# Block attention and a squared-ReLU network on one Trainium2 core: a third buffer for the loaded sums of weights, key and value sums moved to the fifth chunk, exponentials ahead of the high parts, and the last pair's products in another order

## The chip, the core and the metric

The kernel runs on one core of one Trainium2 chip. The core has a matrix engine (TensorE; PE and, for its weight loads, PEld in the profile), a vector engine (VectorE, DVE), an activation engine (ScalarE, ACT), a general one (GpSimd, POOL) and a queue engine that issues transfers (SyncE, SP). The metric is the device time of one execution in microseconds; lower is better.

## The reference, cut to what matters

```
def _attn_ref(q, k, v):                    # 4 x 8 heads x 768 x 64
    k_sum = k.reshape(B, H, nb, 32, D).max(axis=3)
    v_sum = v.reshape(B, H, nb, 32, D).mean(axis=3)
    scores = [local scores inside |i - j| < 16, scores with k_sum + log(32)] * scale
    a = softmax(scores)                    # 96 local keys of a half tile and 24 sums
    return a @ [v, v_sum]

def _moe_ref(x, w_in, w_out):              # x: 3072 x 512, d_ff 2048
    h = np.maximum(x @ w_in, 0.0)
    return h * h @ w_out
```

The attention's output, 3072 rows of 512, is the input x of the two-layer network. All of it is 32-bit.

## The kernel before, in words

The 3072 rows are 24 attention tiles `g` of 128 rows (six to each of the four batches b), and 12 chunks `c` of 256 rows (two tiles each) for the network. Every network product is made of high and low parts (`w_sb[f]` holds both parts of one 128-wide slice f of the two weight matrices; 16 slices), so a first-layer product of one slice is 12 matmuls of 256 columns (`ffn1`, L414 to L422).

Chunks 0 and 1 and the loading and splitting of the weights run in an order written out by hand (`START`). Chunks 2, 3 and 4 (the "slot" chunks) run in eight slots each (`slot`, L506): a slot computes the first layer of two slices into a PSUM bank (`ph`, bank 4 and 5 in turn), then the second layer of the two slices before (`finish`, 24 matmuls at L463), and squares its own result: ScalarE's ReLU (L426) and square (L432), VectorE's product (L437) and the low part (L440), which reads the bank. Chunks 5 to 11 (the "block" chunks, `chunk_blocks`, L682) compute the second layer by block sums that save products (seven block products, `plain` and `summed`, L618 to L621, 21 matmuls at L630 for a pair of slices, in four accumulating banks `acc`). A pair n has its first layer in slot k of its chunk and its block products two slots later, `ffn2_blocks(n - 2)`; the last two pairs' products stand at the chunk's end.

What the block products need beside the weights:

- sums of blocks of the second matrix, made once in the slot chunks on GpSimd (`sums_t`, `split_t`), stored to DRAM (`t_dram`), and loaded anew for each pair by a transfer on GpSimd's queue (`load_t`, L601) into one of two buffers of `t_ring`, pair n into buffer n % 2. In slot k > 1 `load_t(n)` is issued behind `ffn2_blocks(n - 2)`, which read that buffer last; two more are issued at the chunk's end;
- sums of blocks of the squares (`squares_blocks`, `split_blocks`): ReLU, square and the high part on ScalarE (L426, L640, L642), three subtractions on GpSimd (L644, L649, L650), the low part on VectorE (L651), then the high part of the sums on ScalarE (L655) and their low part on GpSimd (L656). They are written to `sets`.

The attention of the next two tiles is spread over the slots of a chunk by lists of steps. In the slot chunks `period(a)` (L524) gives the steps for tiles a and a + 1: `softmax` is VectorE's masked maximum (L315) and ScalarE's exponential (L323) per head, then sum, reciprocal and normalization (L340, L350, L355), then VectorE transposes into `pT` (`turn`, L368). A period starts with the last slot of a chunk (n = 0) and ends with the seventh of the next (n = 7), where TensorE computes the outputs of both tiles (`outputs`, L386): the first into bank 5, the second into bank 4, which holds the slot's own `ph`. Period a = 6 runs in chunk 2, a = 8 in chunk 3, a = 10 in chunk 4.

The keys' and values' sums of batch b + 1 are formed per pair of heads from transposed copies: `load_kv` (two transfers on SyncE's queue, L193 and L194, into a room of the pool tagged "w", which has one room more than the 16 weight slices) and `sum_k`, `sum_v` (VectorE, L197, L202, L205). Batch 2's four pairs stand in periods 8 and 10, batch 3's in chunks 6 and 7. `place_v` (L210) puts the value sums into the last 32 rows of `v_sb` by VectorE transposes (L214) and GpSimd copies (L219, L220); there is one tile `vsum`.

At a chunk's end `evict_blocks` (L658) joins the four banks into the output: a copy of the first bank's half on ScalarE (L664), additions on VectorE (L665 to L672), and four stores on SyncE's queue (L675, L676).

Of the kernel before, what the change touches and what calls it, by code (L numbers as in the profile page):

```python
# [11 lines left out]
F32 = mybir.dt.float32  # L12
F32R = mybir.dt.float32r
# [4 lines left out]
ALU = mybir.AluOpType  # L18
# [6 lines left out]
P = 128  # L25
# [50 lines left out]
def attn_ffn_kernel(ctx: ExitStack, tc: tile.TileContext, q, k, kt, v, vt, v0, w, consts, out, out_rows):  # L76
# [26 lines left out]
    vsum = const.tile([P, NPAIR, 32], F32, name="vsum")  # L103
# [23 lines left out]
    nc.vector.memset(vsum, 0.0)  # L127

    nc.scalar.activation(vsum[:, 0, 0:1], vsum[:, 0, 0:1], AF.Exp)
# [71 lines left out]
    def sum_v(b, p):  # L201
        nc.vector.tensor_reduce(  # L202
            out=vsum[:, p, 0:NB], in_=kv[b, p][:, S : 2 * S].rearrange("a (n j) -> a n j", j=BLOCK), op=ALU.add, axis=AX.X
        )
        nc.vector.tensor_scalar_mul(vsum[:, p, 0:NB], vsum[:, p, 0:NB], 1.0 / BLOCK)  # L205
# [4 lines left out]
    def place_v(g):  # L210
        dst = v_sb[g % 2][96:128]
        if g % 2 == 0:
            for a in range(4):
                nc.vector.transpose(  # L214
                    out=dst[:, 0, :].rearrange("a (p c) -> a p c", c=128)[:, :, a * 32 : a * 32 + 32],
                    in_=vsum[a * 32 : a * 32 + 32],
                )
        else:
            nc.gpsimd.tensor_copy(out=dst[:, 0, :], in_=v_sb[0][96:128, 0, :])  # L219
        nc.gpsimd.tensor_copy(out=dst[:, 1, :], in_=v_sb[0][96:128, 0, :])  # L220
# [302 lines left out]

    def period(a):  # L524
# [28 lines left out]
        if b + 1 < B and t:  # L553
            for n, p in enumerate(((0, 1), (2, 3))[t // 4]):
                last[2 * n].append(lambda p=p: load_kv(b + 1, p))
                after[2 * n + 2].append(lambda p=p: sum_k(b + 1, p))
                after[2 * n + 2].append(lambda p=p: sum_v(b + 1, p))
# [100 lines left out]
    def evict_blocks(c):  # L658
# [4 lines left out]
        p1, p6 = (acc[0][:, i * CT : (i + 1) * CT] for i in range(2))  # L663
        nc.scalar.copy(out=c11, in_=p1)  # L664
# [8 lines left out]
        o = (c - FROM_BLOCKS) * CT  # L673
        for at, x, y in ((o + P, c11, c12), (o, c21, c22)):
            nc.sync.dma_start(out=out_rows[at : at + P, 0:CT], in_=x)  # L675
            nc.sync.dma_start(out=out_rows[at : at + P, CT:], in_=y)  # L676

    def sharpen(g, half):
        add_eps(g, half, nc.vector)
        inverse(g, half)  # L680

    def chunk_blocks(c):  # L682
# [3 lines left out]
        pairs = ((0, 1), (2, 3))[t // 4] if more and b + 1 < B and t else ()  # L686
        early, late = [[] for _ in range(SLOTS)], [[] for _ in range(SLOTS)]
        if more:
            for h in range(2):
                early[0] += [lambda h=h: sharpen(a, h), lambda h=h: norm(a, h, nc.vector)]  # L690
                early[4].append(lambda h=h: sharpen(a + 1, h))
                early[5].append(lambda h=h: norm(a + 1, h, nc.vector))
# [4 lines left out]
            late[3].append(lambda: softmax(a + 1, 0, 4))  # L697
            early[4].insert(0, lambda: softmax(a + 1, 4, 8))
# [13 lines left out]
        for k in range(SLOTS):  # L712
# [11 lines left out]
            if k > 1:  # L724
                load_t(n)
# [154 lines left out]
    with tc.manual_schedule(engines=None):  # L880
# [17 lines left out]
        for c in range(2, FROM_BLOCKS):  # L898
            for f in range(0, NF, 2):
# [84 lines left out]
```

## Time and profile before

| | |
|---|---|
| runs | 605.14, 608.45, 609.23 us; median 608.45 |
| the profiled execution | 608.73 us, of which the span from the first to the last instruction is 606.7 us |
| mean granted clock of TensorE | 0.99 |
| TensorE matmuls / weight loads | 582.5 / 570.5 us busy |
| VectorE, ScalarE, GpSimd | 397.8, 325.2, 340.3 us busy |
| slot chunks 2 to 4 | about 126 to 269 us of the span |
| block chunks 5 to 11 | about 269 to 600 us |

The profile is of one execution. Its page gives busy time per engine, the chain of work that ended last, and groups of instructions by source line; the trace behind it gives waits, timelines and stretches. A row of a timeline has start, duration, engine, line, operation, names written and read, and in brackets how long the engine had been idle and what ended that. Matmuls are pipelined, so a matmul's own duration (275 ns) is longer than the step from one to the next.

### The profile page before, as it was taken

How to read it: one execution, taken by the hardware profiler on the slowest of the kernel's cores; microseconds unless marked ns; L12 is line 12 of the kernel's file. 1: busy time of each engine (PE TensorE's matmuls, PEld its weight loads, DVE VectorE, ACT ScalarE, POOL GpSimd, SP SyncE). 2: the span in 40 equal slices, each digit the busy share in tenths (PEclk: the TensorE clock that was granted, in tenths of full speed). 3: DMA queues.
4: the chain of work that ended last, by engine and by line, in shares of the span. 5: the costliest groups of instructions: out<-in, count | busy, mean ns of one | idle time of the engine just before them, and what ended most of it. 6: DMA issues, size and time to landing. Idle time of an engine off the chain costs nothing.

```text
span 606.7 us, 15592 instructions
## 1 busy us (share of the span) xinstructions
PE 582.5 (96%) x6263; PEld 570.5 (94%) x6263; DVE 397.8 (66%) x1073; ACT 325.2 (54%) x798; POOL 340.3 (56%) x399
## 2 busy tenths in 40 slices
PE   7799999999999999999999899999999999999993
PEld 6699999999999999999999899899999899999993
DVE  6899897977747948947557756675575565663111
ACT  3899756243454443455554644645655654662540
POOL 2546552016625533657756764774783774874871
PEclk9999999999999999999999999999999999999997
DMA  8999702552328219449566847657547646346252
GB/s 302 348 342 419 311 2 94 160 176 70 122 91 275 76 49 312 123 123 278 175 202 199 293 157 238 226 187 251 181 152 224 214 147 206 120 158 223 76 188 87
DMA packets 41799, 114.91 MB, mean 189 GB/s; under 512 B 3776, under 2 KB 20160, under 8 KB 40192
## 3 DMA queue, kind: packets, MB, share of 16 engines
q1 hardware_dynamic: 31488, 67.79, 32.6%
q0 software_dynamic: 10240, 46.14, 23.6%
q8 instruction: 49, 0.80, 0.5%
q14 instruction: 22, 0.18, 0.1%
HBM read 99.24 MB, written 14.68 MB: 188 GB/s over the span
## 4 chain that ended last, share of the span: by engine, by line
PE 65%; POOL 11%; DMA 10%; ACT 5%; DVE 5%; issue 2%; SPq 1%; POOLq 0%; DVEq 0%; ACTq 0%
PE ph L418 27%; PE o_ps L463 16%; PE s_ps L630 8%; DMA t_ring<-t 7%; PE o_ps L630 5%; PE s_ps L418 3%; POOL q_sb L644 3%; POOL sets L656 3%; PE ph L386 3%; POOL q_sb L649 2%; POOL q_sb L650 2%; PE s_ps L287 2%; DMA w_raw<-in_w 2%; ACT r L426 1%; ACT r L640 1%
## 5 line engine op out<-in xcount | busy, mean ns | idle before, releaser
L418 PE MATMUL ph<-x,w_sb 128*128 128x256 f32 x1608 | 192.1, 276 | 0.0
L418 PEld LDWEIGHTS ph<-x,w_sb 128*128 128x128 f32 x1608 | 187.2, 188 | 0.2 <-issue 0.2
L463 PE MATMUL o_ps<-sq,w_sb 128*128 128x256 f32 x960 | 115.4, 275 | 0.2 <-DVE sq L440 0.2
L463 PEld LDWEIGHTS o_ps<-sq,w_sb 128*128 128x128 f32 x960 | 111.7, 188 | 0.5 <-DVE sq L440 0.4
L651 DVE TENSOR_TENSOR sets<-r,sets 128x384 fp32r<-128x384 f32 x56 | 42.2, 754 | 94.6 <-ACT sets L642 91.3
L368 DVE STREAM_TRANSPOSE pT<-e_sb 32x256 f32<-32x256 f32 x228 | 99.4, 436 | 3.9
L426 ACT ACTIVATE r<-ph 128x512 f32<-128x512 f32 x85 | 50.5, 594 | 64.4 <-PE ph L418 60.4
L323 ACT ACTIVATE e_sb<-e_sb,nmx 128x120 f32<-128x120 f32 x176 | 67.8, 389 | 31.5 <-DVE nmx L315 31.5
L656 POOL TENSOR_TENSOR sets<-q_sb,sets 128x512 fp32r<-128x512 f32 x56 | 72.4, 1292 | 20.8 <-ACT sets L655 19.1
L655 ACT CAST sets<-q_sb 128x512 fp32r<-128x512 f32 x56 | 34.8, 622 | 83.6 <-POOL q_sb L650 83.5
L630 PE MATMUL s_ps<-t_ring,sets 128*128 128x256 f32 x336 | 67.6, 282 | 9.3 <-DMA t_ring<-t 9.1
L644 POOL TENSOR_TENSOR q_sb<-r 128x256 f32<-128x256 f32 x56 | 42.1, 751 | 42.7 <-ACT r L640 40.5
L630 PEld LDWEIGHTS s_ps<-t_ring,sets 128*128 128x128 f32 x336 | 51.3, 189 | 11.7 <-DMA t_ring<-t 11.6
L418 PE MATMUL ph<-sq,w_sb 128*128 128x256 f32 x504 | 61.4, 276 | 0.0
L418 PEld LDWEIGHTS ph<-sq,w_sb 128*128 128x128 f32 x504 | 59.0, 188 | 0.5 <-issue 0.5
L630 PE MATMUL s_ps<-w_sb,sets 128*128 128x256 f32 x336 | 57.2, 279 | 0.0
L601 POOL DMA_DIRECT2D t_ring<-t x56 | 31.8, 567 | 36.0 <-PE o_ps L630 26.0
L263 POOL TENSOR_TENSOR w_raw<-w_raw 128x1024 int32<-128x1024 int32 (+1 forms) x20 | 33.2, 1662 | 30.0 <-DVE w_raw L258 12.6
L630 PE MATMUL o_ps<-w_sb,sets 128*128 128x256 f32 x336 | 49.2, 281 | 0.0
L630 PEld LDWEIGHTS s_ps<-w_sb,sets 128*128 128x128 f32 x336 | 47.3, 190 | 0.0
L630 PEld LDWEIGHTS o_ps<-w_sb,sets 128*128 128x128 f32 x336 | 42.9, 188 | 1.4 <-issue 1.0
L437 DVE TENSOR_TENSOR ph<-ph,r 128x512 f32<-128x512 f32 x32 | 22.3, 697 | 28.7 <-ACT r L426 28.4
(121 smaller groups left out, 904.4 us busy)
## 6 DMA issues: line engine op xcount, KB each, us to landing
t_ring<-t POOLq DMA_DIRECT2D x56, 768.0 KB, 4.5
w_raw<-in_w SPq DMA_DIRECT2D x12, 1024.0 KB, 13.7
v_sb<-in_v SPq DMA_DIRECT2D x22, 384.0 KB, 5.1
t<-f SPq DMA_DIRECT2D x16, 512.0 KB, 3.5
k_sb<-in_k SPq DMA_DIRECT2D x19, 384.0 KB, 6.4
kv<-in_kt SPq DMA_DIRECT2D x16, 384.0 KB, 3.8
q_sb<-in_q SPq DMA_DIRECT2D x24, 256.0 KB, 5.3
kv<-in_vt SPq DMA_DIRECT2D x12, 384.0 KB, 4.6
```

The source lines that it names most:

```text
L263: nc.gpsimd.tensor_tensor(out=lo, in0=hi, in1=lo, op=ALU.add)
L323: nc.scalar.activation(e, e, AF.Exp, bias=nmx[g, half][:, i : i + 1], scale=-1.0, accum_out=sm[g, half][:, i : i + 1])
L368: nc.vector.transpose(out=pT[g % 2][j * 32 : j * 32 + 32, :, i * 32 : i * 32 + 32], in_=e_sb[i * 32 : i * 32 + 32, :, j * 32 : j * 32 + 32],)
L418: nc.tensor.matmul(ph, lhsT=w_sb[f][:, w, cc * P : (cc + 1) * P], rhs=x[c][:, cc, :], start=(n == 0), stop=(n == 3 * NC4 - 1))
L426: nc.scalar.activation(r, ph, AF.Relu)
L463: nc.tensor.matmul(o_ps[c][b][:, i * CT : (i + 1) * CT], lhsT=w_sb[f][:, w, d : d + P], rhs=g_, start=(first and n == 0 and i == 0), stop= ...
L601: nc.gpsimd.dma_start(out=t_ring[n % 2], in_=t_dram[n % SLOTS][:, 1:4])
L630: nc.tensor.matmul(acc[b][:, half * CT : (half + 1) * CT], lhsT=operand(n, x, i), rhs=right(n, name, y), start=(first and b not in banks[: ...
L644: nc.gpsimd.tensor_tensor(out=s_flat[:, 0 : 2 * P].rearrange("p (a b) -> p a b", a=2), in0=r0.unsqueeze(1).to_broadcast([P, 2, P]), in1=r[ ...
L651: nc.vector.tensor_sub(out=l, in0=r[:, P:], in1=h.bitcast(F32))
L655: nc.scalar.copy(out=h, in_=s_flat)
L656: nc.gpsimd.tensor_sub(out=l, in0=s_flat, in1=h.bitcast(F32))
```

## The change

Five edits go together:

- A third buffer for the loaded sums of weights, `t_room`, in the pool's one free room. Pair n uses buffer n % 3, slot k > 1 issues `load_t(n + 1)` instead of `load_t(n)`, and a chunk's end issues the loads n + 2 and n + 3.
- So that the room is free by then, all keys' and values' sums of batches 2 and 3 are formed in the slot chunks: a table `keys_values` names for each period the slots at whose end a pair is loaded; its sums stand two slots later. Batch 3's last pair is summed behind the loop. `vsum` becomes two tiles, one for odd and one for even batches.
- In the block chunks all eight masked maxima of tile a + 1 stand at the end of slot 3, and the eight exponentials in two groups of four in slots 4 and 5, each group ahead of that slot's high part of the sums (L655 before).
- `place_v` copies on ScalarE in the block chunks.
- The last pair's products are ordered so that banks 0 and 1 are complete early, and the last chunk's `evict_blocks` has its own form: seven additions of 256 columns, a store behind each finished quarter, the last of them on ScalarE's queue.

```diff
+    vsums = [const.tile([P, NPAIR, 32], F32, name=f"vsum{i}") for i in range(2)]
...
-    def place_v(g):
+    def place_v(g, eng=nc.gpsimd):
...
-            nc.gpsimd.tensor_copy(out=dst[:, 0, :], in_=v_sb[0][96:128, 0, :])
-        nc.gpsimd.tensor_copy(out=dst[:, 1, :], in_=v_sb[0][96:128, 0, :])
+            copy(eng, dst[:, 0, :], v_sb[0][96:128, 0, :])
+        copy(eng, dst[:, 1, :], v_sb[0][96:128, 0, :])
...
+    keys_values = {
+        6: ((2, 2, 0), (4, 2, 1)), 8: ((0, 2, 2), (2, 2, 3)), 10: ((0, 3, 0), (2, 3, 1), (4, 3, 2), (6, 3, 3)),
+    }
...
-        if b + 1 < B and t:
-            for n, p in enumerate(((0, 1), (2, 3))[t // 4]):
-                last[2 * n].append(lambda p=p: load_kv(b + 1, p))
-                after[2 * n + 2].append(lambda p=p: sum_k(b + 1, p))
-                after[2 * n + 2].append(lambda p=p: sum_v(b + 1, p))
+        for n, i, p in keys_values.get(a, ()):
+            last[n].append(lambda i=i, p=p: load_kv(i, p))
+            if n < 6:
+                after[n + 2] += [lambda i=i, p=p: sum_k(i, p), lambda i=i, p=p: sum_v(i, p)]
...
+                t_ring.append(room(F32R, "t_room")[:, 4 : 4 + 6 * CT].rearrange("p (q i n) -> p q i n", q=3, i=2))
-            nc.gpsimd.dma_start(out=t_ring[n % 2], in_=t_dram[n % SLOTS][:, 1:4])
+            nc.gpsimd.dma_start(out=t_ring[n % 3], in_=t_dram[n % SLOTS][:, 1:4])
...
     def ffn2_blocks(n):
+        if n == n_blocks - 1:
+            passes.sort(key=lambda at: (plain + summed[3:] + summed[:3]).index(at[0]))
...
+        if c == n_c - 1:
+            nc.scalar.copy(out=c21, in_=p1)
+            nc.vector.tensor_add(out=c11, in0=acc[1][:, 0:CT], in1=c21)
+            nc.sync.dma_start(out=to[0], in_=c11)
+            nc.vector.tensor_add(out=c22, in0=p6, in1=c21)
+            nc.vector.tensor_add(out=c12, in0=acc[2][:, 0:CT], in1=c22)
+            nc.vector.tensor_add(out=c12, in0=acc[3][:, 0:CT], in1=c12)
+            nc.sync.dma_start(out=to[1], in_=c12)
+            nc.vector.tensor_add(out=c21, in0=acc[2][:, CT:], in1=c22)
+            nc.vector.tensor_add(out=c22, in0=acc[2][:, 0:CT], in1=c21)
+            nc.sync.dma_start(out=to[3], in_=c22)
+            nc.vector.tensor_add(out=c21, in0=acc[3][:, CT:], in1=c21)
+            nc.scalar.dma_start(out=to[2], in_=c21)
+            return
...
-                early[4].append(lambda h=h: sharpen(a + 1, h))
-                early[5].append(lambda h=h: norm(a + 1, h, nc.vector))
...
-            late[3].append(lambda: softmax(a + 1, 0, 4))
-            early[4].insert(0, lambda: softmax(a + 1, 4, 8))
+            late[3] += [lambda h=h: mask_max(a + 1, h) for h in range(H)]
+            for n in range(2):
+                early[4 + n] += [lambda h=h: exponentials(a + 1, h) for h in range(4 * n, 4 * n + 4)]
+            for h in range(2):
+                early[4 + h] += [lambda h=h: sharpen(a + 1, h), lambda h=h: norm(a + 1, h, nc.vector)]
...
-            for n, p in enumerate(pairs):
-                late[(0, 3)[n]].append(lambda p=p: load_kv(b + 1, p))
-                (late[2] if n == 0 else early[4]).extend([lambda p=p: sum_k(b + 1, p), lambda p=p: sum_v(b + 1, p)])
             if b and t == 0:
-                late[4] += [lambda: place_v(a), lambda: place_v(a + 1)]
+                late[4] += [lambda: place_v(a, nc.scalar), lambda: place_v(a + 1, nc.scalar)]
...
             if k > 1:
-                load_t(n)
+                load_t(n + 1)
...
-        load_t(n + 1)
         load_t(n + 2)
+        load_t(n + 3)
...
+        sum_k(3, 3)
+        sum_v(3, 3)
         softmax(2 * FROM_BLOCKS + 2, 0, H)
-        load_t(0)
-        load_t(1)
+        for n in range(3):
+            load_t(n)
```

Three places of the instruction order, before and after. On VectorE, the end of chunk 4: slots 5, 6 and 7 of its period (product and low part L437 and L440, which are L438 and L441 after the change; transposes into `pT_82`), then the low part of x and the chunk's last slot. Before:

```order
L368 STREAM_TRANSPOSE pT_82<-e_sb 32x8x32 x5
L437 TENSOR_TENSOR ph<-ph,r 128x512
L440 TENSOR_TENSOR sq<-ph,sq 128x512
L368 STREAM_TRANSPOSE pT_82<-e_sb 32x8x32 x7
L437 TENSOR_TENSOR ph<-ph,r 128x512
L440 TENSOR_TENSOR sq<-ph,sq 128x512
L403 TENSOR_TENSOR x<-ph,x 128x4x128 x2
```

The same place after the change, with `ksum_87` and `vsum_84` the sums of batch 3:

```order
L369 STREAM_TRANSPOSE pT_82<-e_sb 32x8x32 x5
L438 TENSOR_TENSOR ph<-ph,r 128x512
L441 TENSOR_TENSOR sq<-ph,sq 128x512
L369 STREAM_TRANSPOSE pT_82<-e_sb 32x8x32 x3
L198 TENSOR_REDUCE ksum_87<-kv 128x24
L203 TENSOR_REDUCE vsum_84<-kv 128x24
L206 TENSOR_SCALAR vsum_84<-vsum_84 128x24
L369 STREAM_TRANSPOSE pT_82<-e_sb 32x8x32 x4
L438 TENSOR_TENSOR ph<-ph,r 128x512
L441 TENSOR_TENSOR sq<-ph,sq 128x512
L404 TENSOR_TENSOR x<-ph,x 128x4x128 x2
```

One pair's sums now stand between the third and the fourth of the seven transposes, ahead of the last slot's product and low part. Chunk 2 has the same new rows there, and another pair's sums two slots before.

On GpSimd, slots 2 to 4 of the first block chunk, chunk 5 (`t2_106` is the DRAM copy of the sums of slice pair 2 of 0 to 7, `t3_107` that of pair 3, and so on; `q_sb2_79` takes the sums of squares). Before:

```order
L650 TENSOR_TENSOR q_sb2_79<-r_84,q_sb2_79 128x128
L601 DMA t_ring_3623<-t2_106 128x1536
L656 TENSOR_TENSOR sets_3676<-q_sb2_79,sets_3676 128x512
L644 TENSOR_TENSOR q_sb2_79<-r_84 128x256
L649 TENSOR_TENSOR q_sb2_79<-r_84,q_sb2_79 128x128
L650 TENSOR_TENSOR q_sb2_79<-r_84,q_sb2_79 128x128
L601 DMA t_ring_3623<-t3_107 128x1536
```

The same slots after the change, where the copy of pair 2 is named `t2_108`, that of pair 3 `t3_109`, that of pair 4 `t4_110`:

```order
L657 TENSOR_TENSOR q_sb2_79<-r_85,q_sb2_79 128x128
L606 DMA t_ring_3649<-t3_109 128x1536
L663 TENSOR_TENSOR sets_3704<-q_sb2_79,sets_3704 128x512
L651 TENSOR_TENSOR q_sb2_79<-r_85 128x256
L656 TENSOR_TENSOR q_sb2_79<-r_85,q_sb2_79 128x128
L657 TENSOR_TENSOR q_sb2_79<-r_85,q_sb2_79 128x128
L606 DMA t_ring_3649<-t4_110 128x1536
```

In each slot the load is that of the next pair; pair 2's has moved ahead of the chunk, behind those of pairs 0 and 1.

On TensorE, the last pair's products (`o_ps` are banks 0 and 1 of the four, `s_ps` banks 2 and 3). Before:

```order
L630 MATMUL o_ps<-w_sb,sets 128x256 x6
L630 MATMUL s_ps<-t_ring,sets 128x256 x3
L630 MATMUL s_ps<-w_sb,sets 128x256 x4
L630 MATMUL s_ps<-t_ring,sets 128x256 x2
L630 MATMUL o_ps<-t_ring,sets 128x256 x2
L630 MATMUL s_ps<-w_sb,sets 128x256 x2
L630 MATMUL s_ps<-t_ring,sets 128x256
L630 MATMUL o_ps<-t_ring,sets 128x256
```

And after:

```order
L637 MATMUL o_ps<-w_sb,sets 128x256 x6
L637 MATMUL s_ps<-t_ring,sets 128x256 x3
L637 MATMUL o_ps<-t_ring,sets 128x256 x3
L637 MATMUL s_ps<-w_sb,sets 128x256 x6
L637 MATMUL s_ps<-t_ring,sets 128x256 x3
```

The last product into banks 0 and 1 was the 21st and is now the 12th.

## Rows read from the trace of the kernel before

**Rows 1.** The page: busy time by engine; a group (count, busy us, mean ns, idle us).
```profile
PE 582.5 (96%) x6263; PEld 570.5 (94%) x6263; DVE 397.8 (66%) x1073; ACT 325.2 (54%) x798; POOL 340.3 (56%) x399
...
L630 PEld LDWEIGHTS s_ps<-t_ring,sets 128*128 128x128 f32 x336 | 51.3, 189 | 11.7 <-DMA t_ring<-t 11.6
```

**Rows 2.** Waits of weight loads: total us, times, longest us.
```profile
PEld s_ps L630 <- DMA t_ring<-t: 11.6, 12, 2.3
```

**Rows 3.** Chain that ended last, chunk 6: start us, us, what.
```profile
345.19 1.77 PE s_ps L630 x9
...
348.24 3.26 PE ph L418 x24
...
352.20 1.02 PE s_ps L630 x9
...
353.90 2.73 PE ph L418 x24
```

**Rows 4.** Two stretches: length, busy us by engine, PEclk, DMA share, GB/s.
```profile
345.84:349.26 3.42, 3.42 (x18) 3.42 (x17) 3.37 (x6) 0.88 (x2) 2.49 (x5) 0.50 0.63 246
20.98:23.36 2.38, 0.38 (x18) 0.12 (x6) 1.68 (x13) 2.20 (x12) 1.96 (x2) 1.00 1.01 384
```

**Rows 5.** Instructions by tile `t_ring`, the line on its transfers.
```profile
DMA to landing us min/median/max: 4.3/4.5/8.6
```

**Rows 6.** Timeline of GpSimd, chunk 6, two successive loads.
```profile
332.91 0.57 POOL L601 DMA_DIRECT2D t_ring<-t  x1
...
337.01 0.57 POOL L601 DMA_DIRECT2D t_ring<-t  x1
```

**Rows 7.** Timeline of the end, all engines.
```profile
594.21 0.84 PE L630 MATMUL o_ps<-w_sb,sets 128*128 128x256 f32 x6
...
597.18 0.62 PE L630 MATMUL s_ps<-t_ring,sets 128*128 128x256 f32 x3 [2.13 <-DMA t_ring<-t]
...
599.34 0.41 PE L630 MATMUL o_ps<-t_ring,sets 128*128 128x256 f32 x1
599.79 0.37 ACT L664 COPY q_sb<-o_ps 128x256 f32<-128x256 f32 x1 [6.55 <-PE o_ps L630]
600.20 0.42 DVE L665 TENSOR_TENSOR q_sb<-o_ps,q_sb 128x256 f32<-128x256 f32 x1 [8.47 <-ACT q_sb L664]
...
603.75 0.46 SPq L676 DMA_DIRECT2D out<-q_sb  x1
```

**Rows 8.** Groups by line and shape from 125 us on: count, busy us, mean ns, idle us.
```profile
L197 DVE TENSOR_REDUCE ksum<-kv 128x24 f32<-128x768 f32 x8 | 7.6, 944 | 0.1
L202 DVE TENSOR_REDUCE vsum<-kv 128x24 f32<-128x768 f32 x8 | 7.5, 942 | 0.0
```

**Rows 9.** Timeline of VectorE (chunks 2, 3) and of TensorE (chunk 2's end).
```profile
149.81 0.70 DVE L437 TENSOR_TENSOR ph<-ph,r 128x512 f32<-128x512 f32 x1 [1.58 <-ACT r L426]
...
163.35 0.69 DVE L440 TENSOR_TENSOR sq<-ph,sq 128x512 fp32r<-128x512 f32 x1
...
164.48 2.08 PE L386 MATMUL ph<-pT,v_sb 128*64 128x64 f32 x64
...
195.81 0.70 DVE L437 TENSOR_TENSOR ph<-ph,r 128x512 f32<-128x512 f32 x1 [1.58 <-ACT r L426]
...
211.69 0.69 DVE L440 TENSOR_TENSOR sq<-ph,sq 128x512 fp32r<-128x512 f32 x1
```

**Rows 10.** Timeline of TensorE and of VectorE, chunk 4's end.
```profile
260.06 2.08 PE L386 MATMUL ph<-pT,v_sb 128*64 128x64 f32 x64
...
260.22 0.69 DVE L440 TENSOR_TENSOR sq<-ph,sq 128x512 fp32r<-128x512 f32 x1
```

**Rows 11.** Timeline of GpSimd and of VectorE, chunk 4.
```profile
247.23 2.41 POOL L587 TENSOR_TENSOR f<-f 128x1024 fp32r<-128x1024 f32 x1 [0.49 <-ACT f L586]
...
247.91 2.25 DVE L355 TENSOR_TENSOR e_sb<-e_sb,sm 128x480 f32<-128x480 f32 x1
```

**Rows 12.** Instructions by tile `kv`, the line on its transfers.
```profile
DMA to landing us min/median/max: 3.0/4.2/14.5
```

More of the change, by code (lines that the diff above doesn't have):

```diff
@@ L102, in attn_ffn_kernel @@
     pT = [const.tile([P, H, P], F32, name=f"pT{i}") for i in range(2)]
-    vsum = const.tile([P, NPAIR, 32], F32, name="vsum")
+    vsums = [const.tile([P, NPAIR, 32], F32, name=f"vsum{i}") for i in range(2)]
     r_sb = const.tile([P, 2, CT], F32, name="r")
@@ L125, in attn_ffn_kernel @@
     bank = [ps_s.tile([P, DM], F32, name=n, tag=f"{n}{i}") for i, n in enumerate(["s_ps"] * 4 + ["ph"] * 2)]
-    nc.vector.memset(vsum, 0.0)
-    nc.scalar.activation(vsum[:, 0, 0:1], vsum[:, 0, 0:1], AF.Exp)
+    for t_ in vsums:
+        nc.vector.memset(t_, 0.0)
+    nc.scalar.activation(vsums[1][:, 0, 0:1], vsums[1][:, 0, 0:1], AF.Exp)
     nc.vector.memset(bank[0][:, 3 * P + NK : 3 * P + NK + 4], 1.0e-9)
@@ L202, in sum_v @@
         nc.vector.tensor_reduce(
-            out=vsum[:, p, 0:NB], in_=kv[b, p][:, S : 2 * S].rearrange("a (n j) -> a n j", j=BLOCK), op=ALU.add, axis=AX.X
+            out=vsums[b % 2][:, p, 0:NB], in_=kv[b, p][:, S : 2 * S].rearrange("a (n j) -> a n j", j=BLOCK), op=ALU.add, axis=AX.X
         )
-        nc.vector.tensor_scalar_mul(vsum[:, p, 0:NB], vsum[:, p, 0:NB], 1.0 / BLOCK)
+        nc.vector.tensor_scalar_mul(vsums[b % 2][:, p, 0:NB], vsums[b % 2][:, p, 0:NB], 1.0 / BLOCK)
     def place_k(g, eng=nc.vector):
         copy(eng, k_sb[g % 2][:, 4], ksums[g // NT % 2].unsqueeze(1).to_broadcast([P, 2, NPAIR, NB]))
-    def place_v(g):
+    def place_v(g, eng=nc.gpsimd):
         dst = v_sb[g % 2][96:128]
@@ L215, in place_v @@
                     out=dst[:, 0, :].rearrange("a (p c) -> a p c", c=128)[:, :, a * 32 : a * 32 + 32],
-                    in_=vsum[a * 32 : a * 32 + 32],
+                    in_=vsums[g // NT % 2][a * 32 : a * 32 + 32],
                 )
         else:
-            nc.gpsimd.tensor_copy(out=dst[:, 0, :], in_=v_sb[0][96:128, 0, :])
-        nc.gpsimd.tensor_copy(out=dst[:, 1, :], in_=v_sb[0][96:128, 0, :])
+            copy(eng, dst[:, 0, :], v_sb[0][96:128, 0, :])
+        copy(eng, dst[:, 1, :], v_sb[0][96:128, 0, :])
     w_raw = {}
@@ L611, in right @@
         if name[0] == "t":
-            return t_ring[n % 2][:, int(name[1]) - 2, i, :]
+            return t_ring[n % 3][:, int(name[1]) - 2, i, :]
         j, row, col = n % SLOTS, int(name[1]), int(name[2])
@@ L663, in evict_blocks @@
         p1, p6 = (acc[0][:, i * CT : (i + 1) * CT] for i in range(2))
+        o = (c - FROM_BLOCKS) * CT
+        to = [out_rows[at : at + P, x : x + CT] for at in (o + P, o) for x in (0, CT)]
+        if c == n_c - 1:
[12 more added lines that the diff above has]
+            return
         nc.scalar.copy(out=c11, in_=p1)
@@ L672, in evict_blocks @@
         nc.vector.tensor_add(out=mid, in0=acc[3], in1=mid)
[L673 to L676, printed above, removed]
+        for at, x in zip(to, (c11, c12, c21, c22)):
+            nc.sync.dma_start(out=at, in_=x)
     def sharpen(g, half):
@@ L685, in chunk_blocks @@
         b, t = divmod(a, NT)
-        pairs = ((0, 1), (2, 3))[t // 4] if more and b + 1 < B and t else ()
         early, late = [[] for _ in range(SLOTS)], [[] for _ in range(SLOTS)]
```

## The prediction

> **What bounds the kernel now.** I read the page's busy shares first. TensorE carries matmuls in 96% of the span and weight loads in 94% [rows 1], no other engine is over 66%: time is won only where TensorE stands still, or after its last product. So the second view is the list of waits of TensorE's weight loads. Behind the start-up one group matters: 12 waits, 11.6 us, for the loads of the sums of weights into `t_ring`, the longest 2.3 us [rows 2]. The rest of that list belongs to the start-up or is small. A load took 4.3 to 8.6 us to land, median 4.5 [rows 5].
>
> The third view is the chain that ended last, around one of these waits. At 345.19 us the products start late; they and the next 24 first-layer matmuls end at 348.24 + 3.26 = 351.50, so 6.31 us for 39 matmuls. The same 39, one pair later, take from 352.20 to 353.90 + 2.73 = 356.63, or 4.43 us [rows 3]. The difference of 1.9 us is the clock: from 345.84 to 349.26 the granted clock was 0.50, that is 1.2 instead of 2.4 GHz [rows 4]. The same rows give the pace: 2.73 us for 24 matmuls, 0.114 us each. A pair in the block chunks is 24 + 21 = 45 of them, 5.1 us; a slot in the chunks before is 24 + 24 = 48, 5.5 us.
>
> The last view is the timeline of the end. The last pair's products begin at 594.21, stop for the last load (2.13 us on the matmul row), end at 599.34 + 0.41 = 599.75; then come a ScalarE copy, five VectorE additions and four stores, the last issued at 603.75 [rows 7], 2.95 us before the span's end at 606.7.
>
> **The change, part by part.**
>
> *Third buffer.* Each load is issued one pair earlier, with the same products freeing its buffer (pair n - 2 at the time of pair n; three buffers instead of two). The load whose lateness is seen at 345.19 was issued at 337.01; it would go where the one before it went, at 332.91 [rows 6]. In the middle of a chunk the lead grows by a whole pair of 5.1 us or, as here, where GpSimd catches up, by 4.1 us. The longest wait is 2.3 us [rows 2], so all twelve go. On GpSimd the number of loads is the same and each still stands behind the same products of TensorE; nothing new waits there. A weight load lasts 0.19 us [rows 1] and the next starts 0.11 us after it, so each wait costs 0.075 us more than its idle row shows: 11.6 + 12 x 0.075 = 12.5 us. With it goes the half clock after 345.19: 1.9 us by the matmul rows, of which 0.2 us is already in the weight loads' wait (2.11 there against 1.91 for matmuls), so 1.7. After the last wait, 597.18 to 599.75 is 2.57 us for 15 matmuls that take 14 x 0.114 + 0.28 = 1.87 at the full clock: 0.7 us.
>
> *The last pair.* Its products write banks 0 and 1 whole within the first 12 of 21 instead of at the end, so the copy and two of the additions run beside the last nine (1.0 us). The other five additions of 256 columns cost about 0.45 us each (0.42 by the row of such an addition, and its start). With the products ending at 594.21 + 20 x 0.114 + 0.28 = 596.8, banks 0 and 1 are done at 595.8; copy 0.4, seven additions 3.15: 599.35. The last store, on ScalarE's queue, goes with the 2.95 us of the old last store: 602.3. The tail behind the products becomes 5.5 us instead of 606.7 - 599.75 = 6.95: 1.4 us less. Bounds: 0.5, if every addition waits for the last product, and 1.9, if the first additions that read banks 2 and 3 run early too.
>
> *Sums of keys and values.* Eight pairs instead of four are now loaded and summed in chunks 2 to 4, none in chunks 6 and 7. One pair costs VectorE 944 + 942 ns [rows 8] and a short scaling of 24 columns, some 2.1 us. In chunks 6 and 7 VectorE is idle enough that nothing is won on the path. In chunks 2 and 4 it is not hidden. The two tiles' products with the values stand at a chunk's end; the second tile's write bank 4, which VectorE's L440 of the chunk's seventh slot has to have read. In chunk 4 that subtraction runs from 260.22 to 260.91, and the second 32 matmuls are due 1.04 us after 260.06: 261.1 [rows 10]. There is 0.2 us of slack, and VectorE goes from transposes to this product without a gap. The new sums stand among the transposes just before, so L440 ends at 263.0: TensorE waits 1.9 us.
>
> In chunk 2 two pairs are new. Chunk 3 has had one in the same place, and there the stretch from slot 4's product to the last L440 is 211.69 - 195.81 = 15.88 us, in chunk 2 without it 163.35 - 149.81 = 13.54 [rows 9]. So chunk 2 becomes 15.88 + 2.1: L440 at 167.8, done at 168.5, while the second tile is due at 164.48 + 1.04 = 165.5. That is 3.0 us. Chunk 3 changes nothing. The waits' bounds are 0 (VectorE catches up) and 2.1 for each of the three new pairs before a chunk's end, 6.3 us; I take 4.9. The fourth pair (3, 3) comes behind chunk 4's loop, ahead of the block chunks' first softmax, where the next thing asked of VectorE and ScalarE are the operands of the first block pair, due only after two more pairs' first layers (2 x 2.7 us); they cover it. If not, at most 2.1 us are due.
>
> Does the clock fall at these two waits? It fell after waits of 1.91 and 2.13 us on the matmul rows [rows 3, 7], yet between 20.98 and 23.36, with TensorE busy for 0.38 of 2.38 us, it stayed at 1.00 [rows 4]. One fall costs 1.7 us, so 0 to 3.4; I take one.
>
> A rule of the Trainium skill speaks against moving this work: its page "SBUF — State Buffer", section "SBUF: two separate sides", says that VectorE's operations with two SBUF inputs and GpSimd's that read SBUF share one port pair, and that whichever starts first holds it for the whole instruction. The trace agrees at one place: a normalization (L355) began at 247.91 beside GpSimd's L587 (247.23 to 249.64) and took 2.25 us [rows 11]. By that rule chunk 2's two normalizations, 2 us later, would fall beside GpSimd's shorter subtractions; if that makes the wait there 0.7 us longer (an estimate), the sum below is 599.7, without it 599.0.
>
> *Exponentials ahead of high parts, copies on ScalarE.* ScalarE does the same eight exponentials a tile, now without waiting for VectorE between them, in two pairs' slots. The three copies of value sums in chunks 5 and 8 leave GpSimd for ScalarE. By the copy of 256 columns in 0.37 us [rows 7] 512 columns take at most 0.74 us, 2.2 us in all behind VectorE's transposes. ScalarE then runs late by about 4 us once, but its results are due two pairs (10 us) later, and it catches up. I cost this at nothing, 0 to 1 us.
>
> **The sum**, against the profiled execution's 608.73 us (span 606.7; 0.28 over the median of 608.45): 608.73 - 12.5 - 1.7 - 0.7 - 1.4 + 4.9 + 1.7 = 599.0 us.
>
> **Rivals.**
> 1. *VectorE catches up; chunks 2 and 4 wait for nothing.* For: it idles in the middle of each of these chunks (the 1.58 us before 149.81). Against: it has no gap behind slot 5, and in chunk 4 only 0.2 us of slack [rows 10]. Time: 599.0 - 4.9 - 1.7 = 592.4.
> 2. *Loads stay late.* The third buffer gives lead but not bandwidth; loads slow from 4.5 to 8.6 us where transfers overlap [rows 5]. For half of the waits to stay they would have to take over 5 us longer still. Against: the key and value loads leave chunks 6 and 7, and the load behind the longest mid-run wait, issued at 337.01 and awaited until 345.19, is one of chunk 6 [rows 3, 6]. Time: 599.0 + 6.2 = 605.2.
> 3. *Slower: the room for keys and values serializes the chunks before.* There is one free room, so each of the eight loads waits on SyncE's queue for the sum before it, with the loads of queries and keys and the stores of weight sums behind it. The sum is two slots (10.9 us) after the issue. Landings of `kv` took up to 14.5 us, median 4.2 [rows 12]. If every one took 14.5, VectorE would stand 3.6 us before each of eight sums and TensorE would pay most of 28.8 us: 599.0 + 0.8 x 28.8 = 622. It decides for slower when the landings are over 13 us; the 14.5 was at the start, with the DMA engines full.
> 4. *The change does nothing*, because the loads are held by something other than the buffer: 608 us. Against: the instruction order has each load one pair earlier on GpSimd, behind the same wait.
>
> **How the numbers follow.** My case 0.58, rival 1 0.22, rival 2 0.13, rival 3 0.03, rival 4 0.04. About 1% is what a measurement of this kernel can tell from no change, so faster means under 602.4. My case alone lies between 596.0 (small waits, no fall of the clock) and 602.5 (6.3 us of waits, two falls, half of the tail's gain); rival 1 pulls the low end of the range to 591.0, and most of rival 2 is left out above 604.0. Faster: 0.56 + 0.22 + 0.06 = 0.84; slower 0.03; the rest 0.13.
>
> **What would show it.** Right: no wait of weight loads for `t_ring` or `t_room`; last store's issue 5 to 6 us before the span's end counted from the last product, not 7; a wait of TensorE at the second tile's products (L387) of 3 us in chunk 2 and 2 us in chunk 4, ended by VectorE's L441. Wrong: those two waits missing (rival 1), `t_ring` waits left (rival 2), VectorE's L198 waiting for `kv` (rival 3), or new waits in the block chunks for `sets`, which I expect nowhere.

## The result, and the profile after

The changed kernel takes 599.47 us (median of four runs, 597.92 to 601.78) beside 608.06 us for the kernel before (a fourth run of it came to the three): ratio 0.9869, 95% interval 0.9821 to 0.9917. The profiled execution took 597.92 us, its span 596.1.

The page's busy shares, which answer to [rows 1]:

```profile
PE 577.2 (97%) x6263; PEld 566.8 (95%) x6263; DVE 399.2 (67%) x1076; ACT 328.0 (55%) x804; POOL 334.7 (56%) x393
```

TensorE still bounds the kernel. The waits of its weight loads (total us, times, longest us), where [rows 2] stood:

```profile
PEld ph L387 <- DVE sq L441: 2.5, 1, 2.5
PEld ph L387 <- POOL f L587: 2.4, 1, 2.4
...
PEld o_ps L464 <- DVE sq L441: 1.4, 2, 0.9
...
PEld o_ps L464 <- ACT sq L433: 0.4, 1, 0.4
```

No row for `t_ring` or `t_room` is left. Two waits of some 2.4 us at the second tile's products with the values (L387) are new, and smaller ones at the second layer (L464). The first group below is one of the `t_ring` loads (count, busy us, mean ns, idle us), the two lines under it are the landings of `t_ring` and `t_room` ([rows 5]):

```profile
L637 PEld LDWEIGHTS s_ps<-t_ring,sets 128*128 128x128 f32 x228 | 34.3, 188 | 0.0
...
DMA to landing us min/median/max: 4.4/4.6/7.6
...
DMA to landing us min/median/max: 4.4/4.5/9.0
```

The loads are as slow as before; they start a pair earlier. TensorE's timeline in chunks 2 to 4 shows the price (in brackets: idle before the row, and what ended it), from the scores behind the start-up on:

```profile
124.83 1.05 PE L288 MATMUL s_ps<-k_sb,q_sb 64*64 64x120 f32 x32 [0.26 <-DVE k_sb L140]
...
157.62 2.11 PE L464 MATMUL o_ps<-sq,w_sb 128*128 128x256 f32 x16 [0.69 <-DVE sq L441]
...
165.10 1.15 PE L387 MATMUL ph<-pT,v_sb 128*64 128x64 f32 x32
168.53 1.15 PE L387 MATMUL ph<-pT,v_sb 128*64 128x64 f32 x32 [2.27 <-POOL f L587]
...
254.84 1.21 PE L464 MATMUL o_ps<-sq,w_sb 128*128 128x256 f32 x8 [0.24 <-ACT sq L433]
256.35 2.09 PE L464 MATMUL o_ps<-sq,w_sb 128*128 128x256 f32 x16 [0.30 <-DVE sq L441]
...
263.81 1.15 PE L387 MATMUL ph<-pT,v_sb 128*64 128x64 f32 x32
267.29 1.15 PE L387 MATMUL ph<-pT,v_sb 128*64 128x64 f32 x32 [2.33 <-DVE sq L441]
```

The 64 products that were one row in [rows 9, 10] fall into two halves with a gap. VectorE at the same places:

```profile
162.63 0.95 DVE L198 TENSOR_REDUCE ksum<-kv 128x24 f32<-128x768 f32 x1
163.50 0.94 DVE L203 TENSOR_REDUCE vsum<-kv 128x24 f32<-128x768 f32 x1
164.47 0.62 DVE L206 TENSOR_SCALAR vsum<-vsum 128x24 f32<-128x24 f32 x1
165.10 1.80 DVE L369 STREAM_TRANSPOSE pT<-e_sb 32x256 f32<-32x256 f32 x4
166.93 0.70 DVE L438 TENSOR_TENSOR ph<-ph,r 128x512 f32<-128x512 f32 x1
167.74 0.69 DVE L441 TENSOR_TENSOR sq<-ph,sq 128x512 fp32r<-128x512 f32 x1
...
250.12 2.42 DVE L206 TENSOR_SCALAR vsum<-vsum 128x24 f32<-128x24 f32 x1
...
253.25 0.66 DVE L356 TENSOR_TENSOR e_sb<-e_sb,sm 128x480 f32<-128x480 f32 x1
...
263.19 0.71 DVE L206 TENSOR_SCALAR vsum<-vsum 128x24 f32<-128x24 f32 x1
...
266.54 0.69 DVE L441 TENSOR_TENSOR sq<-ph,sq 128x512 fp32r<-128x512 f32 x1
```

Sums, transposes and the last two products stand without a gap; chunk 2's last subtraction (L441) ends at 167.74 + 0.69 = 168.43, TensorE goes on at 168.53. The list names GpSimd's L587 there, which ended at 168.16 (below); experiment 3 shows that it was VectorE. The 24-column scaling (L206), shortest 0.18 us, took 2.42 us at 250.12. GpSimd at both places:

```profile
167.43 0.73 POOL L587 TENSOR_TENSOR f<-f 128x256 f32<-128x256 f32 x1
...
250.09 2.41 POOL L591 TENSOR_TENSOR f<-f 128x1024 fp32r<-128x1024 f32 x1 [1.52 <-ACT f L590]
```

The same pair was summed at this place before, where its scaling began 0.21 us ahead of GpSimd's subtraction of 247.23 [rows 11] and was short:

```profile
247.02 0.18 DVE L205 TENSOR_SCALAR vsum<-vsum 128x24 f32<-128x24 f32 x1
```

There the normalization behind it took the 2.25 us of [rows 11]; now it takes 0.66. So the hold has changed its victim: 2.24 us more for the scaling, 1.59 less for the normalization, net 0.65 us on VectorE.

The end, which answers to [rows 7]:

```profile
589.51 0.84 PE L637 MATMUL s_ps<-w_sb,sets 128*128 128x256 f32 x6
589.71 0.37 ACT L674 COPY k_sb<-o_ps 128x256 f32<-128x256 f32 x1 [2.04 <-PE o_ps L637]
...
590.19 0.50 PE L637 MATMUL s_ps<-t_ring,sets 128*128 128x256 f32 x3
590.45 0.41 DVE L677 TENSOR_TENSOR q_sb<-o_ps,k_sb 128x256 f32<-128x256 f32 x1
...
593.12 0.37 ACTq L685 DMA_DIRECT2D out<-k_sb  x1
```

The copy now starts beside the last products; from their end at 590.69 to the span's end are 5.41 us. So the two profiled executions can be laid side by side, in us:

| stretch | before | after | difference |
|---|---|---|---|
| start to the end of chunk 4's products with the values | 262.14 | 268.44 | +6.30 |
| from there to the end of the last product | 337.61 | 322.25 | -15.36 |
| tail, to the end of the span | 6.95 | 5.41 | -1.54 |
| outside the span | 2.03 | 1.82 | -0.21 |
| sum | 608.73 | 597.92 | -10.81 |

### The profile page after: what moved, and what is told of

It reads as the page before. It is cut to its first block, busy times and chain, and to the rows that moved or that the text cites. A ratio compares the mean times of both kernels' runs of the same rounds, so it can differ in the third digit from the quotient of the medians.

```text
span 596.1 us, 15599 instructions
## 1 busy us (share of the span) xinstructions
PE 577.2 (97%) x6263; PEld 566.8 (95%) x6263; DVE 399.2 (67%) x1076; ACT 328.0 (55%) x804; POOL 334.7 (56%) x393
## 5 line engine op out<-in xcount | busy, mean ns | idle before, releaser
L464 PE MATMUL o_ps<-sq,w_sb 128*128 128x256 f32 x960 | 115.8, 276 | 1.2 <-DVE sq L441 1.0
L464 PEld LDWEIGHTS o_ps<-sq,w_sb 128*128 128x128 f32 x960 | 111.9, 188 | 1.9 <-DVE sq L441 1.4
L658 DVE TENSOR_TENSOR sets<-r,sets 128x384 fp32r<-128x384 f32 x56 | 44.5, 795 | 88.7 <-ACT sets L649 88.6
L637 PE MATMUL s_ps<-t_ring,sets 128*128 128x256 f32 x228 | 44.2, 276 | 0.0
L438 DVE TENSOR_TENSOR ph<-ph,r 128x512 f32<-128x512 f32 x32 | 22.3, 697 | 28.6 <-ACT r L427 28.3
L316 DVE CUSTOM_DVE_ANT_0 e_sb<-s_ps,c_sb 128x120 f32<-128x120 f32 x176 | 39.6, 274 | 0.2
L656 POOL TENSOR_TENSOR q_sb<-r,q_sb 128x128 f32<-128x128 f32 x56 | 36.5, 653 | 4.4
```

Of the source, the lines that this page charges most:

```text
L316: nc.vector.tensor_tensor_reduce(out=e_of(g)[:, h, 0:NK], in0=s_ps[g][h % 2][:, h // 2, 0:NK], in1=m, scale=-scale, scalar=3.0e38, op0=ALU ...
L464: nc.tensor.matmul(o_ps[c][b][:, i * CT : (i + 1) * CT], lhsT=w_sb[f][:, w, d : d + P], rhs=g_, start=(first and n == 0 and i == 0), stop= ...
L637: nc.tensor.matmul(acc[b][:, half * CT : (half + 1) * CT], lhsT=operand(n, x, i), rhs=right(n, name, y), start=(first and b not in banks[: ...
L656: nc.gpsimd.tensor_sub(out=s2, in0=r2, in1=s0)
L658: nc.vector.tensor_sub(out=l, in0=r[:, P:], in1=h.bitcast(F32))
```

## The experiments

The theory: the third buffer alone takes the loads' waits away; the sums of keys and values give part of it back, because VectorE's queue has no room for them where they stand. Every kernel below was timed against the kernel before on the same chip. The ratios come from that; the kernel before had medians of 606.76, 607.45 and 606.91 us on the three chips of the experiments and 608.06 on the first, so medians of different kernels compare to 1 to 2 us only. Each kernel's trace is read at three places: from the start of the scores behind the start-up (124.83 in the changed kernel) to the end of chunk 4's products with the values, "chunks 2 to 4"; from there to the end of the last product, "blocks"; and the tail. That start itself lies at 123.47 to 126.32 us and belongs to no edit.

| kernel | median us | ratio to before, 95% | chunks 2 to 4 | blocks | tail |
|---|---|---|---|---|---|
| before | 608.06 | | 136.94 | 337.61 | 6.95 |
| changed | 599.47 | 0.9869 (0.9821 to 0.9917) | 143.61 | 322.25 | 5.41 |
| sums_only | 615.56 | 1.0145 (1.0077 to 1.0212) | 145.43 | 340.28 | 6.97 |
| ring_and_sums | 601.35 | 0.9899 (0.9862 to 0.9935) | 144.95 | 323.36 | 7.02 |
| no_sums | 590.93 | 0.9741 (0.9718 to 0.9763) | 136.46 | 322.22 | 5.42 |
| sums_idle | 594.25 | 0.9797 (0.9774 to 0.9820) | 138.83 | 322.21 | 5.40 |
| scale_late | 595.37 | 0.9811 (0.9781 to 0.9841) | 140.90 | 322.22 | 5.37 |
| sums_idle_scale_late | 591.17 | 0.9751 (0.9723 to 0.9778) | 136.65 | 322.22 | 5.32 |
| pieces | 597.20 | 0.9840 (0.9796 to 0.9884) | 142.13 | 322.21 | 5.30 |
| old_tail | 601.70 | 0.9908 (0.9872 to 0.9944) | 145.42 | 322.22 | 6.94 |
| old_steps | 598.44 | 0.9860 (0.9828 to 0.9892) | 144.49 | 322.22 | 5.32 |

Every trace with three buffers has blocks of 322.2 us, but for the one in which the clock fell at their border. What differs lies ahead of them or behind.

**1. sums_only: the new place of the sums, nothing else.**

```diff
-        if b + 1 < B and t:
...
+        for n, i, p in keys_values.get(a, ()):
+            last[n].append(lambda i=i, p=p: load_kv(i, p))
+            if n < 6:
+                after[n + 2] += [lambda i=i, p=p: sum_k(i, p), lambda i=i, p=p: sum_v(i, p)]
...
-        pairs = ((0, 1), (2, 3))[t // 4] if more and b + 1 < B and t else ()
+        pairs = ()
```

> The kernel before with one edit of the change alone: keys' and values' sums of batches 2 and 3 formed by the fifth chunk, two buffers as before, old tail. Theory A (the third buffer brings the gain, the new place of the sums costs what the new waits in chunks 2 and 4 show, about 3.3 + 3.0 us): the 12 waits for t_ring stay at about 11 us, the waits at the products with the values come on top, time 608 + 6 = about 614 us. Rival B (the loads of weight sums were late because key and value loads stood beside them in chunks 6 and 7, so moving those is half of the gain): the waits for t_ring there fall, the sum of these waits is under 7 us, time 604 to 609 us.

Measured: 615.56 us (four runs, 611.11 to 619.27), ratio 1.0145: slower than before by itself. TensorE's weight loads:

```profile
PEld s_ps L634 <- DMA t_ring<-t: 13.8, 10, 2.7
PEld ph L387 <- POOL f L587: 3.0, 1, 3.0
...
PEld ph L387 <- DVE sq L441: 2.0, 1, 2.0
```

The waits for the loads are no shorter than before (11.6 us in 12), though no load of keys or values stands in their chunks. Rival B falls, and with it half of the prediction's second rival: transfers crowded by keys and values were not the reason.

**2. ring_and_sums: the third buffer on top of that.**

```diff
+                t_ring.append(room(F32R, "t_room")[:, 4 : 4 + 6 * CT].rearrange("p (q i n) -> p q i n", q=3, i=2))
-            nc.gpsimd.dma_start(out=t_ring[n % 2], in_=t_dram[n % SLOTS][:, 1:4])
+            nc.gpsimd.dma_start(out=t_ring[n % 3], in_=t_dram[n % SLOTS][:, 1:4])
...
             if k > 1:
-                load_t(n)
+                load_t(n + 1)
```

> The kernel of the first experiment (sums of keys and values by the fifth chunk, 615.6 us) and the third buffer, nothing else of the change: softmax steps, copies and tail as before. Theory A (the third buffer alone brings the gain in the block chunks): no wait for t_ring or t_room, and the time falls by the 13.8 us of those waits and by a clock fall or two of 1.7 us, 615.6 - 14 = about 601.5 us, the time of the kernel with the old tail (601.7). Rival H (the buffer needs ScalarE's and GpSimd's new order as well, since the operands would be late next): waits for sets appear, 603 us or more.

Measured: 601.35 us, 14.2 less; no wait for `t_ring`, `t_room` or `sets`. On top of the moved sums the buffer is the whole gain in the blocks, without the other softmax order, and rival H falls. (The buffer without the moved sums was not run; it takes the room that their loads would need.) In this trace the clock fell behind both new waits of chunks 2 and 4, which are 2.28 and 2.12 us on the matmul rows, beside 2.27 and 2.33 in the changed kernel. The stretches at the half clock (length, busy us by engine, PEclk, DMA share, GB/s):

```profile
169.51:172.93 3.42, 3.42 (x65) 3.12 (x62) 0.69 (x1) 0.51 (x1) 0.00 (x0) 0.50 0.02 5
268.50:271.91 3.41, 3.41 (x57) 2.99 (x53) 0.69 (x2) 1.53 (x2) 1.77 (x3) 0.50 0.32 73
```

and stretches of the same length right behind the waits of the changed kernel:

```profile
168.53:171.95 3.42, 3.42 (x100) 3.19 (x101) 1.19 (x2) 0.59 (x1) 0.00 (x0) 1.00 0.02 5
267.29:270.71 3.42, 3.42 (x75) 3.19 (x76) 1.23 (x2) 1.53 (x2) 0.60 (x1) 1.00 0.39 81
```

A stretch of 3.42 us at the half clock loses 1.71 us. Of the five traces that keep the sums in the change's slots with their scalings and GpSimd's work as it was, the clock fell behind chunk 2's wait in four (this kernel and sums_only, old_tail, old_steps) and stayed at 1.00 in the changed kernel's. That wait was 2.83 to 2.85 us in sums_only, old_tail and old_steps, so only this trace and the changed kernel's compare equal waits. Less 1.71 us for each fall (0.51 for the part of this trace's second one), chunks 2 to 4 take 142.7 to 143.7 us in the five traces, by this estimate: single traces of the same slots differ by 1 us.

**3. no_sums: the changed kernel without these sums.** The loads stay; batches 2 and 3 use the sums of batches 0 and 1.

```diff
-            if n < 6:
-                after[n + 2] += [lambda i=i, p=p: sum_k(i, p), lambda i=i, p=p: sum_v(i, p)]
...
-        sum_k(3, 3)
-        sum_v(3, 3)
```

> The changed kernel without the sums of keys and values of chunks 2 to 4 on VectorE (the loads stay; batches 2 and 3 use the sums of batches 0 and 1). Theory A: the waits of TensorE at the values' products of chunks 2 and 4 (2.4 and 2.3 us) and the small ones of 0.2 to 1.0 us before them go, and chunk 4 loses the 0.5 us it also had before: 599.5 - 6.3 = about 593 us, the price of the sums. Rival C (behind VectorE stands ScalarE or GpSimd, which is late at the same place): waits of 1 us or more remain there with another releaser, time 596 to 599 us.

Measured: 590.93 us, 2 less than expected. The products with the values of chunk 4 are one row again, as in [rows 10]:

```profile
259.88 2.08 PE L387 MATMUL ph<-pT,v_sb 128*64 128x64 f32 x64
```

Nothing else is late there; rival C falls. So does GpSimd's L587 as the cause of chunk 2's wait: in this trace the same subtraction runs from 168.36 us on, when that chunk's products with the values, begun at 164.77, are done. Chunks 2 to 4 take 136.46 instead of 143.61 us: the price of the sums is 7.15 us here (6.3 to 7.3 by the five traces above), of which the kernel before paid 0.5 us too (136.94 - 136.46). By the medians it is 8.5 us; the changed kernel's other three runs had a mean clock of 0.992 to 0.993 where the profiled one had 0.998, so falls of the clock may be in it.

**4. sums_idle: the same sums in other slots.**

```diff
-        6: ((2, 2, 0), (4, 2, 1)), 8: ((0, 2, 2), (2, 2, 3)), 10: ((0, 3, 0), (2, 3, 1), (4, 3, 2), (6, 3, 3)),
+        6: ((1, 2, 0, 3), (5, 2, 1, 8)), 8: ((0, 2, 2, 2), (2, 2, 3, 4), (4, 3, 0, 8)),
+        10: ((0, 3, 1, 2), (2, 3, 2, 4), (4, 3, 3, 8)),
...
+            if m == 3:
+                before[m] += both
+            elif m < 8:
+                after[m] += both
+            else:
+                last[7].append(lambda both=both: due.extend(both))
```

Behind each pair stands the slot of its sums; 8 means the first slot of the next period, which is the chunk's last slot, and not the next chunk as the expectation below has it.

> The changed kernel with the same sums in other slots: ahead of slot 3's products, in slots 2 and 4, and at the start of the next chunk, where VectorE idles, instead of slots 4 to 7. Theory A: it is the place on VectorE's queue that costs, so the waits at the values' products in chunks 2 and 4 fall under 0.5 us each and the time is 599.5 - 5 = about 594.5 us. Rival D (it is the amount of work in the chunk that costs, wherever it stands): VectorE is late by the same 2 us per pair at the chunk's end, time 598 to 600 us.

Measured: 594.25 us, both L387 waits gone, though chunk 2 still sums two pairs: most of the price is the place and not the amount, and rival D falls. What remains of it, 138.83 - 136.46 = 2.4 us, is in waits at L464 (2.1 us on the weight loads' rows), the longest here:

```profile
147.36 2.12 PE L464 MATMUL o_ps<-sq,w_sb 128*128 128x256 f32 x16 [1.00 <-DVE sq L441]
```

and VectorE just ahead of it, behind the scaling of the pair that now stands ahead of slot 3's products:

```profile
143.47 2.44 DVE L206 TENSOR_SCALAR vsum<-vsum 128x24 f32<-128x24 f32 x1
145.83 0.68 DVE L438 TENSOR_TENSOR ph<-ph,r 128x512 f32<-128x512 f32 x1
146.62 0.69 DVE L441 TENSOR_TENSOR sq<-ph,sq 128x512 fp32r<-128x512 f32 x1
```

GpSimd's long subtraction began 0.02 us earlier:

```profile
143.45 2.42 POOL L598 TENSOR_TENSOR f<-f 128x1024 fp32r<-128x1024 f32 x1 [1.17 <-ACT f L597]
```

**5. scale_late: the scaling once a batch.** The sums stay in the change's slots.

```diff
     def sum_v(b, p):
...
-        nc.vector.tensor_scalar_mul(vsums[b % 2][:, p, 0:NB], vsums[b % 2][:, p, 0:NB], 1.0 / BLOCK)
...
         if g % 2 == 0:
+            vs = vsums[g // NT % 2]
+            nc.vector.tensor_scalar_mul(vs[:, :, 0:NB], vs[:, :, 0:NB], 1.0 / BLOCK)
```

> The changed kernel with the scaling of the values' sums by 1/32 taken out of each pair's sums and done once a batch ahead of the transposes that place them; the sums stay in their slots. Theory E (scalings that begin beside a GpSimd instruction last as long as it): in chunk 4 2.42 + 0.71 us and in chunk 2 0.18 + 0.62 us go from VectorE's queue, the waits at the values' products fall by about 2.5 us in chunk 4 and 0.8 us in chunk 2, 596 us. Rival F (only the reductions' 0.94 us each matter): under 1 us less, 598.5 to 599.5 us.

Measured: 595.37 us. Chunks 2 to 4 are 2.7 us shorter than in the changed kernel. The L387 waits are 1.66 and 1.59 us on the matmul rows instead of 2.27 and 2.33. Rival F falls. The split was not as expected: with those at L464 the waits fell from 2.96 to 1.83 us in chunk 2 and from 2.87 to 1.59 us in chunk 4, not by 0.8 and 2.5.

**6. pieces: one edit on GpSimd, none on VectorE.**

```diff
-        nc.gpsimd.tensor_sub(out=t_sb.bitcast(F32R), in0=t_sb, in1=t_high)
+        for o in range(0, 4 * CT, CT):
+            nc.gpsimd.tensor_sub(out=t_sb[:, o : o + CT].bitcast(F32R), in0=t_sb[:, o : o + CT], in1=t_high[:, o : o + CT])
```

> The changed kernel with one edit on GpSimd alone: its subtraction of 1024 columns (2.41 us) that stood beside the 2.42 us scaling is four of 256 columns. Theory E: the scaling lasts no longer than such a piece, 0.2 to 0.8 us, though VectorE's own queue is unchanged, and chunk 4's waits (0.5 + 0.6 + 2.5 us) fall by 1.6 to 2.2 us: about 597.5 us. If the 2.42 us were VectorE's own (a drain behind the reductions): the scaling stays at 2.4 us and the time at 599.5 us.

The edit cuts all eight such subtractions. Measured: 597.20 us, which its interval doesn't tell from the changed kernel's. The trace decides on the scaling. VectorE and, under it, GpSimd at the place where the scaling took 2.42 us:

```profile
249.82 0.75 DVE L206 TENSOR_SCALAR vsum<-vsum 128x24 f32<-128x24 f32 x1
```

```profile
249.79 3.27 POOL L592 TENSOR_TENSOR f<-f 128x256 fp32r<-128x256 f32 x4 [0.48 <-ACT f L590]
```

Four pieces in 3.27 us; the scaling lasts about as long as one. Its length is set by the GpSimd instruction beside it, not by VectorE. Chunks 2 to 4 are 1.5 us shorter (142.13 instead of 143.61), but only 0.6 us under the shortest of the five estimates above. And the L387 wait of chunk 4, which was to shrink, stays at 2.47 us, since the pair of sums at that chunk's end is untouched. That part of the expectation was wrong.

**7. sums_idle_scale_late: the two together.**

> As the one before, and the scaling of the values' sums by 1/32 taken out of each pair's sums and done once a batch, ahead of the transposes that place them. Theory E (a scaling of 0.18 us takes up to 2.42 us when it begins beside a GpSimd instruction): eight such scalings go from the queue, 0 to 1 us less than the one before, 593.5 to 594.5 us. If the scaling costs nothing on the path once the sums stand where VectorE idles: the same time within 0.3 us.

Measured: 591.17 us, ratio 0.9751 (0.9723 to 0.9778), faster than both kernels and within 0.3 us of the one without sums. Theory E had the sign right and the size too small: 3.1 us less than experiment 4 by the medians and 2.2 in chunks 2 to 4, not 0 to 1. Chunk 4's products with the values:

```profile
259.67 2.09 PE L388 MATMUL ph<-pT,v_sb 128*64 128x64 f32 x64
```

**8. old_tail: the last pair and the end as before.**

```diff
-        if n == n_blocks - 1:
-            passes.sort(key=lambda at: (plain + summed[3:] + summed[:3]).index(at[0]))
...
-        if c == n_c - 1:
-            nc.scalar.copy(out=c21, in_=p1)
...
-            return
```

> The changed kernel with the last pair's products and the last additions and stores in the order of before. Prediction's step: the tail behind the last product is 6.95 instead of 5.5 us, 1.4 us more, about 601 us. Bounds 0.5 and 1.9.

Measured: 601.70 us, 2.2 more by the medians, whose spreads are 2.5 and 3.9 us; by the traces 6.94 - 5.41 = 1.53. Its last product and last store:

```profile
593.68 0.28 PE L635 MATMUL o_ps<-t_ring,sets 128*128 128x256 f32 x1
...
597.95 0.45 SPq L681 DMA_DIRECT2D out<-q_sb  x1
```

**9. old_steps: softmax order and copies as before.**

```diff
-            late[3] += [lambda h=h: mask_max(a + 1, h) for h in range(H)]
-            for n in range(2):
-                early[4 + n] += [lambda h=h: exponentials(a + 1, h) for h in range(4 * n, 4 * n + 4)]
+            late[3].append(lambda: softmax(a + 1, 0, 4))
+            early[4].append(lambda: softmax(a + 1, 4, 8))
...
-                late[4] += [lambda: place_v(a, nc.scalar), lambda: place_v(a + 1, nc.scalar)]
+                late[4] += [lambda: place_v(a), lambda: place_v(a + 1)]
```

> The changed kernel with the block chunks' softmax steps in the order of before and the copies of value sums on GpSimd. Prediction's step: nothing (0 to 1 us): no wait of TensorE in the block chunks, 599.5 us. Rival G (these steps keep ScalarE's or GpSimd's results from being late once the loads no longer are): waits for sets in chunks 5 and 8, 601 us or more.

Measured: 598.44 us, blocks 322.22 us as with the change: the two edits neither cost nor bring anything there. Rival G falls.

## Why the prediction was right

The forecast was 599.0 us, the measurement 599.47; faster, and in the likeliest case's own range. The terms, by the stretches of the first table:

- *Third buffer, -12.5, -1.7 and -0.7 us.* -15.36 in the two traces, -14.2 by the medians of experiments 1 and 2, for -14.9. The medians' figure is loose, with runs of sums_only 8 us apart. All twelve waits are gone, no `sets` wait took their place, and every trace with three buffers has the blocks at 322.2 us, but for the one with a fall at their border. Of the second rival (loads stay late) nothing is left.
- *The last pair, -1.4 us.* -1.54 between the profiled executions, 1.53 by undoing it. The tail of 5.5 us is 5.41.
- *Sums of keys and values, +4.9 us.* The place, the mechanism and the releaser were right: L441 of chunk 2 was to end at 168.5 and ended at 168.43, or 168.8 on the clock of the trace before, which begins these chunks 0.37 us later. The size was the mis-sized term: +6.67 in chunks 2 to 4 (143.61 - 136.94), 0.4 beyond the bound of 6.3; by the five traces of experiment 2 it is 5.8 to 6.8, above 4.9 in each. The step that failed is the 1.9 us for chunk 4, where TensorE's idle rows are 0.24 + 0.30 + 2.33 = 2.9 us. It priced a pair at 944 + 942 ns and a short scaling, 2.1 us; the scaling at that chunk's end took 0.71 instead of 0.18 us, and behind the hold in its middle the waits at L464 were 0.54 us. They are 0.19 us in the trace before and in ring_and_sums', where the scaling in the middle took 0.18 us. In chunk 2 TensorE also stopped 0.69 us for L464, which was not foreseen; with the 2.27 us at L387 that is 2.96, for the 3.0 forecast.
- *The clock, +1.7 us.* One fall was assumed; behind the new waits the profiled run has none, ring_and_sums two, sums_only, old_tail and old_steps one. It depends on the run. The three slower runs of the changed kernel have mean clocks of 0.992 to 0.993; traces with one fall ahead of the tail show 0.997 (no_sums, old_steps), with two 0.991 (ring_and_sums, old_tail), so one or two falls each would fit, which no trace of theirs shows. The two misses, +1.8 and -1.7, cancel in the profiled sum, and that is luck; the remaining 1.1 us is the blocks, the tail, the start-up and the time outside the span.
- *Exponentials and copies, 0.* Experiment 9.
- *The rule on the port pair* was brought in for chunk 2's normalizations, 0.7 us. The first of them took 1.23 us instead of 0.66, the second 0.66 as before. GpSimd also holds the scaling, 2.42 instead of 0.18 us, which the prediction overlooked: it named operations with two inputs, and the scaling has one. The Trainium skill's page "SBUF — State Buffer", section "SBUF: two separate sides", has VectorE's operations in a two-port mode, or with two SBUF inputs, contend with GpSimd's for one port pair, and whichever starts first holds it for the whole instruction. Experiment 6 agrees with such a hold: 2.42 us beside one subtraction of 2.41, 0.75 us beside a piece of about that length. In which mode the scaling ran, no run shows.
- *Rival 3* (rooms serialize): the landings of keys and values in chunks 2 to 4 took 3.0 to 6.3 us, not over 13, and L198 waited for none of them. *Rival 1* (VectorE catches up) fell with the two waits, but experiment 7 is a kernel in which it does: 591.17 us for its 592.4.

## What to carry to other kernels

A deeper buffer pays the waits it removes, with the clock falls behind them, if the transfer's issue can go earlier: here moving other traffic out of the way brought nothing by itself. Before work is moved to an engine with a low busy share, look for the places in the stage where it has gaps; the sums cost 7.15 us in the change's slots and 2.4 in others, and of the latter 2.2 went with the small scalings. And count a small instruction by what runs beside it: those scalings, 0.18 us each alone, were worth 2.7 of the 7.15 us in the two traces compared.

## What the runs showed of the hardware

- A VectorE scaling of 24 columns lasted 0.18 us at the shortest. Where it began beside a GpSimd addition or subtraction, it ended with that one: 0.62 us from 164.47 to 165.09, with GpSimd's addition of 512 columns (L583) ending at 165.05; 0.71 us beside a subtraction of 256 columns (0.73 us); 2.42 and 2.44 us where it began 0.02 to 0.03 us after one of 1024 columns. In ring_and_sums it began 0.22 us ahead of that subtraction and took 0.18 us; the normalization behind it then took 2.26. The reductions right ahead of it (0.94 to 0.95 us) show no such spread.
- An idle of 2.27 us at one place left TensorE's clock at 1.00 in one trace, and one of 2.28 us at the same place brought it to 0.50 in another. In these chunks the longest idle without a fall was 2.47 us (pieces), the shortest with one 2.12 (ring_and_sums). What decides it stays open; one kernel's single trace doesn't price such a wait.
